# Paired score search in two early slots, and four steps moved in the opening of a fused top-k attention and feed-forward kernel

## The chip, the cores and the metric

The kernel runs on one core of a Trainium2 chip, as one launch. The metric is the device time of that launch in microseconds; lower is better.

## The reference

Top-k attention over 8 batches of 8 heads (sequence 576, head size 64) feeds a feed-forward layer over the 4608 resulting rows. All in float32.

```python
scores = scale * np.matmul(q, k.transpose(0, 1, 3, 2))        # (8, 8, 576, 576), scale = 1/8
kth = np.partition(scores, -32, axis=-1)[..., -32:-31]        # the 32nd largest of each row
scores = np.where(scores >= kth, scores, -1e9)
attn = np.exp(scores - scores.max(-1, keepdims=True))
attn = attn / (attn.sum(-1, keepdims=True) + 1e-09)
x = np.matmul(attn, v).transpose(0, 2, 1, 3).reshape(4608, 512)
h = x @ w_in                                                  # 512 -> 2048
out = (h * (1 / (1 + np.exp(-1.702 * h)))) @ w_out            # 2048 -> 512
```

## The kernel before

The work is cut into 144 **slots** (`N`), 18 to a batch. A slot is 128 query rows of a pair of heads, so its scores `sc` are 128 partitions x 2 heads x 576 keys; two of the 18 take the last 64 rows of two pairs instead. The order of the instructions on each engine is the order in which the program issues them (a manual schedule); nothing reorders them. Tiles come from rotating pools, so a tile's write waits until the buffer's last user is done: `scp` (4 buffers) holds scores, `raws` (7) raw weight pieces and later `lesser` and `h`, `lefts` (2) the searches' working copies, `ps_t` and `ps_s` (2 each) are in PSUM.

What happens to a slot:

- TensorE multiplies q and k (`scores`, L295); ScalarE copies them out of PSUM, scaled (`copy_scores`, L307).
- VectorE finds the 32nd largest of each row. **Whole** (`topk`, L317 and L320): four rounds of MAX8 (eight largest) and MATCH_REPLACE8 (take them out) over 576 values, for both heads. **Paired** (`topk_of_pairs`, L366 to L378): `pair_up` first takes the larger of key j and key j + 288 into `greater` on VectorE (L336), and GpSimd computes the smaller into `lesser` with integer arithmetic, a subtraction (L339) and, in `pair_rest`, an addition (L349). Four rounds over `greater` and two over `lesser`, 288 values each, and two small reductions (L373, L378) give the same bound.
- GpSimd makes two small values per row: for a whole search `cut` and `low` (L410, L411, in `bounds`), for a paired one `low` alone (L399, in `lows`; `cut` comes from L378).
- ScalarE masks with `cut` (L423) and takes exponentials with `low` (L431), summing into `den`.
- VectorE inverts `den` (`invert`, L439 and L441). In the first slots (`divide`) GpSimd puts the inverse on a diagonal `by` (L448) that TensorE multiplies with while it transposes (`turn_main`, `turn_ends`, L468 and L471, copied out by ScalarE at L476); later (`normalize`) GpSimd multiplies the row (L454), ScalarE splits it into 16-bit halves (`split`, L490) and a DMA transposes it (`turn_by_dma`, L492 and L498).
- TensorE multiplies with v (L526 in `values`, L557 in `values_at`); ScalarE copies x out (L539, or L571 and L574). In the first slots `bring_all` issues those copies that were put off, and then the first multiplication with x.

Four slots with all heads of the same rows make a block of x. A unit of the feed-forward layer is: TensorE's `hidden` (L618), ScalarE's `tanh` (L640, and with `aside` a copy `h`, L643), `gate` on VectorE (L655) or, with `aside`, on GpSimd (L652, L653), and TensorE's `project` (L673), written out by `leave` (L681, L683). Units stand in queues (`to_gate`, `gated`, `to_project`), so a unit is projected some slots after its gate.

The weights are rounded in 32 **pieces** in slots 0 to 11: per piece ScalarE's `size`, `low`, `sign` (L151, L154, L153), VectorE's `shift` (L152), and two GpSimd passes, `add` and `finish` (L144, L147), taken from the list `unfinished` by `finish_one`. `project` reads a piece only once it is finished.

Slots 0 to 10 (`slot(n)`, `SETTLED` = 10) use the whole search, and from slot 11 (`PAIRED`) on `two_slots(n)` does two slots at a time with the paired search: `find` searches, `measure` computes `low`, ends the pair build and gates a unit.

Of the kernel before, what the change touches and what calls it, by code (L numbers as in the profile page):

```python
# [11 lines left out]
F32 = mybir.dt.float32  # L12
# [6 lines left out]
P = 128  # L19
# [11 lines left out]
def kernel(  # L31
# [52 lines left out]
    TURNS = 4  # L84
    SETTLED = 10
    PAIRED = SETTLED + 1
    assert D == 64 and 2 * TAIL == P and C == NP * P and C == PIECE and B % 2 == 0
    assert TOPK == 32 and NP == 4 and NF == 4 and NG == 4 and CC == 4

# [219 lines left out]
    def topk(n):  # L309

        sc = st[n]["sc"]
        top = st[n]["top"] = small.tile([P, 2, TOPK], F32, name="top")
        left = [lefts.tile([P, S], F32, name="left") for _ in range(2)]
        of = lambda r, i: left[i][:] if r else sc[:, i, :]

        def largest(r, i):
            nc.vector.max(top[:, i, 8 * r : 8 * r + 8], of(r, i))  # L317

        def remove(r, i):
            nc.vector.match_replace(left[i][:], top[:, i, 8 * r : 8 * r + 8], of(r, i), LOWEST)  # L320

        ops = []
        for r in range(TOPK // 8):
            ops += [lambda r=r, i=i: largest(r, i) for i in range(2)]
            if r < TOPK // 8 - 1:
                ops += [lambda r=r, i=i: remove(r, i) for i in range(2)]
        return ops
# [3 lines left out]
    def pair_up(n):  # L331

        sc = st[n]["sc"]
        a, b = sc[:, :, 0:HALF], sc[:, :, HALF:S]
        greater[n] = lefts.tile([P, 2, HALF], F32, name="greater", tag="left")
        nc.vector.tensor_tensor(out=greater[n][:], in0=a, in1=b, op=ALU.max)  # L336
        lesser[n] = raws.tile([P, 2, HALF], F32, name="lesser", tag="raw")
        whole = lesser[n][:].bitcast(I32)
        nc.gpsimd.tensor_tensor(out=whole, in0=a.bitcast(I32), in1=greater[n][:].bitcast(I32), op=ALU.subtract)  # L339
        unpaired.append(n)  # L340
# [3 lines left out]
    def pair_rest():  # L344

        while unpaired:
            n = unpaired.pop()
            whole, b = lesser[n][:].bitcast(I32), st[n]["sc"][:, :, HALF:S]
            nc.gpsimd.tensor_tensor(out=whole, in0=whole, in1=b.bitcast(I32), op=ALU.add)  # L349

    def topk_of_pairs(n):

        top = st[n]["top"] = small.tile([P, 2, 2 * TOPK], F32, name="top2", tag="top")
        cut = st[n]["cut"] = small.tile([P, 2], F32, name="cut")
        first, few = greater.pop(n), lesser.pop(n)
        left = lefts.tile([P, 2, HALF], F32, name="left2", tag="left")

        def found(r, i, written=False):
            if r < TOPK // 8:
                at = (8 * r + TOPK) % (TOPK + TOPK // 2)  # L360
                return top[:, i, at : at + 8]
            end = 2 * TOPK - 8 * (r - TOPK // 8) - TOPK
            return top[:, i, end - 1 : end - 9 : -1] if written else top[:, i, end - 8 : end]

        def largest(src, r, i):
            nc.vector.max(found(r, i, True), src[:, i, :])  # L366

        def remove(to, src, r, i):
            nc.vector.match_replace(to[:, i, :], found(r, i), src[:, i, :], LOWEST)  # L369

        def merge():
            both = top[:, :, 0:TOPK].rearrange("p i (s k) -> p i k s", s=2)
            nc.vector.tensor_reduce(  # L373
                out=top[:, :, TOPK + TOPK // 2 :], in_=both, axis=mybir.AxisListType.X, op=ALU.max
            )

        def bound():
            nc.vector.tensor_reduce(  # L378
                out=cut[:], in_=top[:, :, TOPK + TOPK // 2 - 1 :], axis=mybir.AxisListType.X, op=ALU.min, negate=True
            )  # L380

        ops = []
        for r in range(TOPK // 8):
            ops += [lambda r=r, i=i: largest(left if r else first, r, i) for i in range(2)]
            if r < TOPK // 8 - 1:
                ops += [lambda r=r, i=i: remove(left, left if r else first, r, i) for i in range(2)]
        ops += [lambda: pair_up(n + 1) if n + 1 < N else None]
        for r in range(TOPK // 8, TOPK * 3 // 16):
            ops += [lambda r=r, i=i: largest(few, r, i) for i in range(2)]
            if r == TOPK // 8:  # L390
                ops += [lambda r=r, i=i: remove(few, few, r, i) for i in range(2)]
        return ops + [merge, bound]
# [9 lines left out]

    def bounds(n):

        if n >= PAIRED:
            return lows(n)
        top = st[n]["top"]
        cut = st[n]["cut"] = small.tile([P, 2], F32, name="cut")
        low = st[n]["low"] = small.tile([P, 2], F32, name="low")
        nc.gpsimd.tensor_scalar(cut[:], top[:, :, TOPK - 1], -1.0, None, op0=ALU.mult)  # L410
        nc.gpsimd.tensor_tensor(out=low[:], in0=top[:, :, TOPK - 1], in1=top[:, :, 0], op=ALU.subtract)  # L411

    def exponentials(n, between=lambda: None):

        mask(n)
        between()
        exps(n)
# [398 lines left out]
    def slot(n):  # L816

        todo = later.pop(n, [])
        for fn, args in todo:
            if fn is not prepare and fn is not prepare_by_dma:  # L820
                fn(*args)
        preparing = [(fn, args) for fn, args in todo if fn is prepare or fn is prepare_by_dma]
        some = [round_piece(x) for x in by_slot.get(n, [])] if n else early
        if n == 0:
            for piece in some:
                piece["low"]()
                piece["sign"]()
        else:
            bounds(n - 1)
            exponentials(n - 1, bring_all if n % 4 == 1 else lambda: None)  # L830
            copy_scores(n + 1)
            bring_all()
            while signs:
                signs.pop(0)()
            if 1 < n <= TURNS:
                turn_main(n - 2)
                turn_ends(n - 2)
            for piece in some:
                piece["size"]()
            tanh(False)  # L840
        for i, op in enumerate(topk(n)):
            op()
            if i == 2:
                for _ in range(min(3 if n >= TURNS else 6, len(unfinished))):
                    finish_one()
            if i == 5:
                if n > 0:
                    divide(n - 1)
                while unfinished:
                    finish_one()  # L850
            if i == 10:
                gate(False)
        if n == SETTLED:
            pair_up(n + 1)
            pair_rest()
        for piece in some:
            piece["shift"]()
            unfinished.extend(piece["finish"])
        if n < NP:
            for fn, args in preparing:  # L860
                fn(*args)
        if n >= TURNS:
            turn_main(n - 1)
            turn_ends(n - 1)
        if n > 0:
            for piece in some:
                piece["low"]()
        scores(n + 2)
        if n == SETTLED:
            copy_scores(n + 2)  # L870
        if n == 0:
            return
        for i, piece in enumerate(some):
            if n == TURNS and i > 0:
                signs.append(piece["sign"])
            else:
                piece["sign"]()
        idle = not ready and n < TURNS
        if 1 < n <= TURNS:
            values(n - 2, put_off if n == TURNS else None)  # L880
        if n >= TURNS:
            values(n - 1, put_off)
        if n >= NP:
            for fn, args in preparing:
                fn(*args)
        if n > PROJECTS and may_project(2):
            project(n == SETTLED)
        if idle:
            stay_warm(8)
        hidden()  # L890
# [12 lines left out]
    def two_slots(n):  # L903
# [27 lines left out]
        def measure(m):  # L931
            if live(m):
                lows(m)
            pair_rest()
            gate(aside)

        def project_one():
            if may_project(0):
                project(True)

        if opens:
            bounds(n - 1)
            gate(aside)
        if ahead:
            scores(n + 2)
# [26 lines left out]
        for piece in some:  # L972
            piece["shift"]()
            piece["low"]()
            piece["sign"]()
            unfinished.extend(piece["finish"])
        if live(n - 1):
            split(n - 1)
        begin(todo[0])
# [26 lines left out]
        find(n + 1)  # L1006
        if live(n):
            normalize(n)
            split(n)
        begin(todo[1])  # L1010
        if live(n):
# [44 lines left out]
```

## Time and profile before

| | |
|---|---|
| median of 3 runs | 1456.52 us (1456.08 to 1456.63) |
| profiled execution, its own time | 1456.39 us |
| its span in the profile | 1454.6 us |
| mean granted TensorE clock | 0.986 |
| busy: TensorE, VectorE, ScalarE, GpSimd | 1416.5, 1362.5, 1158.9, 977.6 us |
| slot 1 starts on VectorE | 19.72 us |
| slot 11 starts on VectorE | 134.65 us |
| last TensorE wait of over 1 us ends | 224.90 us |

In rows of an engine in order of time, the first number is the start in us, the second the length, then engine, line, operation, what it writes and reads, and in brackets how long the engine had been idle before it and what ended that. Instructions of an engine overlap a little at their ends, so the text takes the step from one start to the next as an instruction's price ("steps"). The time outside the span, 1.79 us here, lies before the first and behind the last instruction.

### The profile page before, as it was taken

Reading aid. Unit: us, or ns where it says so; the run is one execution under the profiler, and the core shown is the slowest. Engines: PE = TensorE matmul, PEld = TensorE weight load, DVE = VectorE, ACT = ScalarE, POOL = GpSimd, SP = SyncE. Lnnn points to the kernel's source line nnn. Section 1 sums busy time; section 2 is a strip of 40 time slices with the busy share of each in tenths; the row PEclk is TensorE's granted clock in tenths of the full one; section 3 lists DMA queues with packets and bytes.
Section 4 is the critical chain, followed back from the end, with each engine's and each line's share of the span. In section 5 each row is a group of like instructions: output and inputs, shape, how many; then the busy total and the mean of one; then the engine's idle time right before and its main releaser. Section 6 shows DMA issues by size and latency. Waiting matters only on the chain.

```text
span 1454.6 us, 29079 instructions
## 1 busy us (share of the span) xinstructions
PE 1416.5 (97%) x9524; PEld 996.4 (68%) x9524; DVE 1362.5 (94%) x4681; ACT 1158.9 (80%) x1862; POOL 977.6 (67%) x1177
## 2 busy tenths in 40 slices
PE   7789799999999999999999999999999999999998
PEld 5667466777666667777666667777666667777665
DVE  7999999999999999999999999999999999999910
ACT  6998787888888887888888888888878888777730
POOL 3788766766677777666777777766777767667610
PEclk8899899999999999999999999999999999999999
DMA  7442467777777867777677767767677776645430
GB/s 224 136 161 75 127 154 191 189 189 180 176 198 184 188 170 191 186 198 177 170 194 182 183 170 195 202 174 189 166 203 189 180 182 179 161 133 130 138 89 15
DMA packets 521272, 244.40 MB, mean 168 GB/s; under 512 B 457376, under 2 KB 495264, under 8 KB 521120
## 3 DMA queue, kind: packets, MB, share of 16 engines
q1 hardware_dynamic: 520688, 242.25, 64.4%
q8 instruction: 75, 1.23, 0.3%
q14 instruction: 77, 0.63, 0.2%
q10 hardware_dynamic: 432, 0.30, 0.1%
HBM read 45.09 MB, written 103.42 MB: 102 GB/s over the span
## 4 chain that ended last, share of the span: by engine, by line
PE 87%; DVE 10%; ACT 2%; POOL 0%; issue 0%; DMA 0%; DVEq 0%; POOLq 0%; ACTq 0%
PE ph L618 33%; PE po L673 32%; PE o L557 10%; PE s_ps L295 10%; DVE top L317 4%; DVE left L320 3%; DVE top L366 1%; DVE left L369 1%; ACT sc L490 0%; ACT sc L423 0%; ACT pr L431 0%; DVE wout L152 0%; PE none L169 0%; ACT sc L307 0%; DMA pt<-rows 0%
## 5 line engine op out<-in xcount | busy, mean ns | idle before, releaser
L618 PEld LDWEIGHTS ph<-xT,win 128*128 128x128 f32 x3520 | 484.2, 191 | 85.2 <-issue 54.6
L618 PE MATMUL ph<-xT,win 128*128 128x128 f32 (+1 forms) x3520 | 537.1, 309 | 0.5 <-ACT xT L574 0.5
L673 PE MATMUL po<-wout,th 128*128 128x512 f32 x1152 | 521.0, 595 | 5.6 <-POOL wout L147 5.6
L490 ACT COPY sc<-pr 128x2304 uint16<-128x2304 uint16 x134 | 283.1, 2113 | 170.3 <-POOL pr L454 170.3
L673 PEld LDWEIGHTS po<-wout,th 128*128 128x128 f32 x1152 | 213.6, 191 | 219.0 <-issue 205.8
L366 DVE MAX8 top<-left 128x8 f32<-128x288 f32 x798 | 323.2, 446 | 0.0
L339 POOL TENSOR_TENSOR lesser<-sc,greater 128x576 int32<-128x576 int32 x133 | 188.4, 1417 | 179.8 <-DVE greater L336 179.8
L454 POOL TENSOR_SCALAR pr<-pr,rden 128x576 f32<-128x576 f32 x268 | 196.6, 746 | 126.7 <-DVE top L373 77.7
L369 DVE MATCH_REPLACE8 left<-top,left 128x288 f32<-128x288 f32 x532 | 231.3, 442 | 0.0
L431 ACT ACTIVATE pr<-sc,low 128x576 f32<-128x576 f32 x288 | 220.8, 774 | 0.0
L366 DVE MAX8 top<-lesser 128x8 f32<-128x288 f32 x532 | 214.9, 445 | 0.0
L423 ACT ACTIVATE sc<-sc,cut 128x576 f32<-128x576 f32 x288 | 207.4, 774 | 6.2 <-POOL cut L410 6.2
L307 ACT ACTIVATE sc<-s_ps 128x576 f32<-128x576 f32 x288 | 170.9, 648 | 34.2 <-PE s_ps L295 32.6
L349 POOL TENSOR_TENSOR lesser<-lesser,sc 128x576 int32<-128x576 int32 x133 | 187.8, 1412 | 0.1
L295 PE MATMUL s_ps<-qk_t 64*128 64x288 f32 (+1 forms) x1280 | 183.7, 433 | 0.5 <-ACT qk_t L218 0.3
L653 POOL TENSOR_TENSOR th<-th,h 128x512 f32<-128x512 f32 x131 | 167.5, 1279 | 10.9
L295 PEld LDWEIGHTS s_ps<-qk_t 64*128 64x128 f32 (+1 forms) x1280 | 100.2, 179 | 79.2 <-issue 59.0
L557 PE MATMUL o<-pt,v_l 128*64 128x128 f32 (+1 forms) x2400 | 145.8, 265 | 2.1 <-DMA pt<-rows 1.9
L557 PEld LDWEIGHTS o<-pt,v_l 128*64 128x64 f32 x2400 | 121.4, 137 | 29.5 <-issue 17.7
L336 DVE TENSOR_TENSOR greater<-sc 128x576 f32<-128x576 f32 x133 | 131.9, 992 | 0.0
L652 POOL TENSOR_SCALAR th<-th 128x512 f32<-128x512 f32 x131 | 81.5, 622 | 59.7 <-ACT th L640 59.7
L640 ACT ACTIVATE th<-ph 128x512 f32<-128x512 f32 x144 | 85.5, 593 | 38.0 <-PE ph L618 33.9
(78 smaller groups left out, 1365.5 us busy)
## 6 DMA issues: line engine op xcount, KB each, us to landing
rows<-sc SPq DMA_DIRECT2D x134, 576.0 KB, 3.2
qk_rows<-halves SPq DMA_DIRECT2D x48, 256.0 KB, 2.8
qk_l<-in_q_dram SPq DMA_DIRECT2D x64, 128.0 KB, 3.4
raw<-in_moe_w_in_dram SPq DMA_DIRECT2D x16, 512.0 KB, 4.7
v_l<-in_v_dram SPq DMA_DIRECT2D x32, 256.0 KB, 3.7
raw<-in_moe_w_out_dram SPq DMA_DIRECT2D x16, 512.0 KB, 3.5
out_dram<-ob SPq DMA_DIRECT2D x32, 256.0 KB, 2.9
qk_l<-in_k_dram SPq DMA_DIRECT2D x62, 128.0 KB, 3.4
```

The lines of the kernel that those rows point to most:

```text
L295: nc.tensor.matmul(ps[i][rows, c, 0:HALF], lhsT=qT[b, hps[p]][on, cols], rhs=kT[b, hps[p]][on, FIRST[i] + c * HALF : FIRST[i] + (c + 1) * ...
L339: nc.gpsimd.tensor_tensor(out=whole, in0=a.bitcast(I32), in1=greater[n][:].bitcast(I32), op=ALU.subtract)
L349: nc.gpsimd.tensor_tensor(out=whole, in0=whole, in1=b.bitcast(I32), op=ALU.add)
L366: nc.vector.max(found(r, i, True), src[:, i, :])
L369: nc.vector.match_replace(to[:, i, :], found(r, i), src[:, i, :], LOWEST)
L423: nc.scalar.activation(sc[:, i, :], sc[:, i, :], AF.Prelu, bias=cut[:, i : i + 1], alpha=HUGE)
L431: nc.scalar.activation(pr[:, i * S : (i + 1) * S], sc[:, i, :], AF.Exp, bias=low[:, i : i + 1], accum_out=den[:, i : i + 1],)
L454: nc.gpsimd.tensor_scalar(pr[:, i, :], pr[:, i, :], st[n]["rden"][:, i : i + 1], 1.0, op0=ALU.mult, op1=ALU.mult)
L490: nc.scalar.copy(out=halves, in_=pr[:].bitcast(U16).rearrange("p (k h) -> p h k", h=2))
L557: nc.tensor.matmul(o[j * D : (j + 1) * D, cols], lhsT=main[:, j, c, :] if c < NF else tail[:, j, :], rhs=pt[:, MAIN[j] + c if c < NF else ...
L618: nc.tensor.matmul(ph[:, i * many * P : (i + 1) * many * P], lhsT=win[:, c, f * P : (f + 1) * P], rhs=xs[:, first : first + step * (many - ...
L673: nc.tensor.matmul(x.po[:], lhsT=gT[:, i * P : (i + 1) * P], rhs=wout[:, f, :], start=(x.done == 0), stop=(x.done == FC - 1))
```

## The change

Slots 1 and 2 (`EARLY`) use the paired search, with `lesser` in a buffer of `scp`; `bounds` of the slot before a paired one is issued ahead of the pair build, also for slot 10. In those two slots the inversion (`divide`) comes after the eleventh step of the search, and so do the last finishing passes ahead of L448. In slot 5 (`TURNS + 1`) the put-off copies of x come behind the exponentials, not between mask and exponentials, and the gate comes after the last step of the search. In slot 4 (`TURNS`) two of the three `low` steps on ScalarE are issued ahead of the transposes. In the first pair of slots (11, 12) two finishing passes take the place of a gate ahead of the end of the pair build, slot 11's own piece is finished right behind, and the gates follow one slot later. In slot 13 `tanh` is issued ahead of `split`. The order of TensorE's instructions and of SyncE's is not changed.

```diff
+    EARLY = (1, 2)
+    by_pairs = lambda n: n in EARLY or PAIRED <= n < N
...
-        lesser[n] = raws.tile([P, 2, HALF], F32, name="lesser", tag="raw")
+        home, tag = (scp, "sc") if n in EARLY else (raws, "raw")
+        lesser[n] = home.tile([P, 2, HALF], F32, name="lesser", tag=tag)
...
-        ops += [lambda: pair_up(n + 1) if n + 1 < N else None]
+        ops += [lambda: pair_up(n + 1) if PAIRED < n + 1 < N else None]
...
-        if n >= PAIRED:
+        if by_pairs(n):
             return lows(n)
...
-            bounds(n - 1)
-            exponentials(n - 1, bring_all if n % 4 == 1 else lambda: None)
+            if not by_pairs(n):
+                bounds(n - 1)
+            exponentials(n - 1, bring_all if n % 4 == 1 and n > TURNS + 1 else lambda: None)
+            if n == TURNS + 1:
+                bring_all()
...
-        for i, op in enumerate(topk(n)):
+        for i, op in enumerate(topk_of_pairs(n) if n in EARLY else topk(n)):
...
-            if i == 5:
+            if i == (10 if n in EARLY else 5):
                 if n > 0:
                     divide(n - 1)
                 while unfinished:
                     finish_one()
-            if i == 10:
+            if i == (13 if n == TURNS + 1 else 10):
                 gate(False)
-        if n == SETTLED:
+        if by_pairs(n + 1):
+            bounds(n)
             pair_up(n + 1)
             pair_rest()
...
+        lows_of = [piece["low"] for piece in some] if n > 0 else []
+        if n == TURNS:
+            for _ in range(2):
+                lows_of.pop(0)()
         if n >= TURNS:
             turn_main(n - 1)
             turn_ends(n - 1)
-        if n > 0:
-            for piece in some:
-                piece["low"]()
+        for low in lows_of:
+            low()
...
             if live(m):
                 lows(m)
+            if opens and m == n:
+                finish_one()
+                finish_one()
+                pair_rest()
+                return
             pair_rest()
             gate(aside)
+            if m == SETTLED + 4:
+                gate(aside)
...
         if opens:
-            bounds(n - 1)
             gate(aside)
...
             unfinished.extend(piece["finish"])
+        while unfinished:
+            finish_one()
         if live(n - 1):
             split(n - 1)
...
             normalize(n)
+        if n == SETTLED + 3:
+            tanh(aside)
+        if live(n):
             split(n)
```

## The prediction

> **What bounds the kernel now.** I read the page's busy table and its 40 slices first, then the chain that ended last, then each engine in order of time through the first 230 us, since the diff ends at slot 14 (about 185 us).
>
> ```profile
> PE 1416.5 (97%) x9524; PEld 996.4 (68%) x9524; DVE 1362.5 (94%) x4681; ACT 1158.9 (80%) x1862; POOL 977.6 (67%) x1177
> PE   7789799999999999999999999999999999999998
> DVE  7999999999999999999999999999999999999910
> PEclk8899899999999999999999999999999999999999
> PE 87%; DVE 10%; ACT 2%; POOL 0%; issue 0%; DMA 0%; DVEq 0%; POOLq 0%; ACTq 0%
> ```
>
> TensorE is full from the sixth slice on: after 225 us it waits 0.5 us in all. Its instruction order is the same in both kernels, so a gain must come from waits before 225 us, and what is gained there is kept to the end. In the opening VectorE (DVE) carries the chain, slot after slot, with only these two waits in slots 1 to 10:
>
> ```profile
> 68.37 0.17 DVE L439 TENSOR_SCALAR some<-den 128x2 f32<-128x2 f32 x1 [1.06 <-ACT pr L431]
> 72.77 0.69 DVE L655 SCALAR_TENSOR_TENSOR th<-th,ph 128x512 f32<-128x512 f32 x1 [0.54 <-ACT th L640]
> ```
>
> Both are in slot 5. The busy time by slot shows why (first number the length, then PE, PEld, DVE, ACT, POOL): ScalarE (ACT) works 13.22 of 13.30 us in slot 5 and 11.42 of 11.51 in slot 6. It is a second bound right behind DVE.
>
> ```profile
> 63.13:76.43 13.30, 12.07 (x131) 10.39 (x128) 11.66 (x27) 13.22 (x28) 9.24 (x11) 0.99 0.45 146
> 76.43:87.94 11.51, 9.17 (x86) 7.96 (x86) 11.47 (x27) 11.42 (x24) 9.14 (x9) 1.00 0.40 138
> ```
>
> Behind slot 10 the chain goes through GpSimd (POOL) to ACT and back to DVE, and TensorE has its last large gaps:
>
> ```profile
> 156.03 1.41 POOL lesser L339
> 157.44 1.45 POOL pr L454 x2
> 158.91 2.11 ACT sc L490
> ...
> 164.40 0.23 DVE some L439
> ```
> ```profile
> 153.52 2.07 PE L673 MATMUL po<-wout,th 128*128 128x512 f32 x2 [5.07 <-POOL wout L147]
> 156.13 2.07 PE L673 MATMUL po<-wout,th 128*128 128x512 f32 x2 [0.53 <-POOL wout L147]
> 179.50 0.66 PE L217 MATMUL tp<-ident,qk_l 128*128 128x128 f32 x4 [1.01 <-ACT h L643]
> 224.90 1.09 PE L557 MATMUL o<-pt,v_l 128*64 128x128 f32 x16 [1.33 <-DMA pt<-rows]
> ```
>
> **Part 1: paired search in slots 1 and 2.** Slot 1's whole search runs 19.72 to 29.64 us with 0.27 of L439/L441 in it: 9.65. Slot 11's paired search steps 1.57 three times and 0.73 (5.45), then 2.64 for lesser, merge and bound (152.25 to 155.20 less 0.31): 8.09. L336, new in front of it, steps 0.66 with POOL quiet. So 0.90 less per slot, 1.80 for two.
>
> Against it stands POOL. L336 and L439 wait while a POOL instruction runs:
>
> ```profile
> 150.72 1.60 DVE L336 TENSOR_TENSOR greater<-sc 128x576 f32<-128x576 f32 x1
> 160.65 0.74 DVE L336 TENSOR_TENSOR greater<-sc 128x576 f32<-128x576 f32 x1
> ```
>
> The first meets L144 (150.43 to 151.71), the second a free POOL. Following POOL's queue: cut(0) and low(0) end at 20.7 (the shifts L152 hold them back, as at 40.39), L339 and L349 (1.41 each) to 23.5, four piece passes (1.3 each) to 28.8, two L448 to 29.45. lesser is needed at 25.8, so it is covered by 2 us. L439 of slot 1 falls at a seam between pieces (24.7, costs 0.15). At the end of slot 1, L448 delays the second L336 by about 0.3; low(1), behind it and the two shifts, comes at 31.2, half a microsecond after the mask is done, and L339 and L349 after that push the pieces so that slot 2's L439 meets one (0.4 to 0.6). Ends of this cost: 0, or 1.3 for each of two L336 and two L439 (5.2). I take 0.8, near the rows' phase: part 1 brings **-1.0** at the start of slot 3.
>
> The Trainium skill ("SBUF — State Buffer", section "Who interferes with whom") says that a DVE instruction with two SBUF inputs and a GpSimd one that reads SBUF block each other for the whole instruction, which speaks against adding L336 and four passes of 1.41 here. The 1.60 agrees. Were every added pass met whole, part 1 would lose: -1.8 + 4 x 1.41 = +3.8.
>
> **Part 2: slot 5.** Two L154 of slot 4 move ahead of the second turn, where ACT waits 0.59 and 1.12 for TensorE; so the mask starts at 63.9, not 65.0. x's copy (0.37) moves behind the exponentials. Together den is ready at 66.75, and L439 wants it at 67.2: the 1.06 is gone. The gate moves to the last place, 73.2, and tanh is done at 71.7: the 0.54 is gone. **-1.60.** What is late next: x's copy comes 0.7 later, TensorE's L618 behind it starts at 67.15 and ends 70.8, so ACT now waits 0.4 for the transposes, and slot 6's mask starts 76.9 instead of 77.4. DVE has moved by 2.6 there, ACT by 1.5 (0.5 plus the 1.0 of part 1, since slot 4's mask follows DVE's cut). Mask and exponentials take 2.9: den at 76.9 - 1.0 + 2.9 = 78.8, L439 at 80.53 - 2.6 = 77.9. DVE waits: **+0.9** (bounds 0 and 2.3). After that DVE's 11.5 a slot is longer than ACT's 11.05, and the lag shrinks. Sum at slot 11: -1.0 - 1.6 + 0.9 = **-1.7**.
>
> **Part 3: bounds ahead, two pieces ahead of a gate** (times of before, on top of -1.7). bounds(10) ahead of the pair build frees ACT's mask 1.75 earlier (135.96 against 137.71), but the next copy waits for scores at 141.6 anyway: nothing, cover 2.8. On POOL, slot 10's third piece goes ahead of L349 at 147.1 and is done at 149.75 (before: 153.46), slot 11's piece at 154.5 (156.07). The gate (L652, L653, 1.9) goes one slot back. Hence L454 of slot 11 starts at 156.0, not 157.41, L490 at 157.5, and L439, which waited 1.43 at 164.40, does not wait for den. But L336 at 160.2 now meets L653 (160.0 to 161.25) and pays about 0.7. The unit gated late is read only at 183.67, two units lie ahead of it: no wait. Net for DVE **-0.85** (bounds 0 and -1.9).
>
> **Part 4: tanh ahead of the split.** ph is there at 172.95, tanh and h end at 174; L490 waits for L454 until 175.5 anyway, so the split pays nothing (cover 1.5). TensorE loses its 1.01 and stands 1.4 + 1.0 earlier at 187, where pt of slot 13 (DVE -0.85, landing 4.5 after its issue at 183.72) holds it about 0.2. With L490 earlier, L653 leaves L336 at 180.40 alone (1.26 to 0.74), and DVE's wait of 0.88 at 202.80, which goes back to TensorE's L673 through L681, goes too: both stand at about **-2.2** at 209, where DVE waits for TensorE's scores. From there the chain to 224.90 moves as a whole.
>
> On the clock: the profile's 3 us stretches show TensorE granted 1.00 from 90 to 93 us with a wait of 2.09, then 0.69 and 0.74, and 0.50 from 155 to 161 after the 5.07. In its place come gaps of about 1.3 and 2.7, and I leave the slow stretch in; TensorE has 1 us to spare before pt of slot 11 there. "TensorE: Matmul & The Clock Gate" (Part 1) puts the throttle after an idle window of about 3.4 us; the 2.09 does not fit that. By the page TensorE would be some 4 us better off in this stretch, and the sum the same, since DVE is last.
>
> **Sum.** -1.7 - 2.2 = -3.9. The profiled execution took 1456.39 with a span of 1454.6 (1.79 around it): 1452.5. It lies 0.13 under the median 1456.52, from which -3.9 gives 1452.6.
>
> **Rivals.** *ACT keeps the opening.* For it: 11.42 of 11.51 us busy. If low(1), and the exponentials and score copy queued behind it, cost ACT 1.4 us more in slots 2 to 5, slot 6 hands back 2.3 for 0.9, and parts 1 and 2 leave 0.3; with parts 3 and 4 at -1.9 that is -2.2: 1454.3. Against it: the mask of slot 4 is bound by DVE's cut. Chance 0.19, from 0 to -2.9.
> *TensorE, not DVE, sets the way to 225 us*, with no collisions: -1.7 (a full part 1, 0.1 kept back), -1.6, +0.8, and -3.5 (1.5 + 1.0 + 0.45 at L222 + part of the 1.33): -6.0, 1450.5. Against it: DVE is busy 9.57 of 9.67 at 175 to 184. Chance 0.14.
> *Slower: DVE falls into another rhythm with POOL.* From 290 to 1380 us L336 alternates 1.25 and 0.74 in each pair of slots of 18.87, and in stretches of 100 us DVE is 98.2 to 99.1 busy: 0.2 idle a pair. If a changed phase makes both 1.25, it owes 0.51 - 0.2 = 0.3 in each of 61 pairs: +19, less 4: 1471. It decides as soon as the second L336 of a pair meets more than 0.2 of a POOL pass. Against it: the last reduce L378 leads TensorE's next scores by 1.4 us at 300 and 1.7 at 1200, so the rhythm is set by TensorE. Chance 0.07.
> That an edit does nothing: the order of the instructions shows them all in place; part 4 alone could be idle, which is inside the range.
>
> **How the numbers follow.** The sum holds: 0.60, from -2.9 to -5.2, 1451.3 to 1453.6. A change under 0.2%, 2.9 us, is about what a measurement of this kernel cannot tell from none. Faster by more: 0.60 + 0.14 = 0.74; within: 0.19; slower: 0.07. The range goes from -6.3 to -1.2: it leaves out the slow rival, the low end of ACT's (0.06) and the far end of TensorE's (0.03).
>
> **What would show it.** Right: no wait at L439 and L655 in slot 5, one of about 1 us at L439 in slot 6; slot 11's L366 near 133 instead of 134.65; wout waits of under 3 us; no wait at L217 near 176; TensorE full from about 221. Wrong: L439 or L336 of slots 1 and 2 over 1 us; ACT waits in slots 5 to 7 that DVE pays for; L336 at 1.25 twice in a pair after 225.

## The result, and the profile after

| | before | after |
|---|---|---|
| median | 1456.57 us (1456.05 to 1457.44, 12 runs) | 1452.59 us (1452.07 to 1453.72, 12 runs) |
| profiled execution, its own time | 1456.39 us | 1453.04 us |
| its span | 1454.6 us | 1451.2 us |

The ratio is 0.9974, with a 95% interval of 0.9965 to 0.9982: 3.98 us faster, inside the predicted range and 0.01 us from the predicted time. The way there is not quite the predicted one: the opening gave 0.7 more than the sum had, and a late transfer at 241 us took 0.9 of it back in the profiled execution.

The page of the changed kernel first (lines have moved down by two or three: L336 is L338, L378 is L381, L431 is L434, L439 is L442, L557 is L560, L655 is L658, L673 is L676):

```profile
PE 1414.1 (97%) x9524; PEld 995.2 (69%) x9524; DVE 1361.8 (94%) x4703; ACT 1159.9 (80%) x1862; POOL 985.2 (68%) x1181
PE   7889899999999999999999999999999999999998
DVE  7999999999999999999999999999999999999910
PEclk8999999999999999999999999999999999999999
PE 85%; DVE 11%; ACT 1%; DMA 1%; SPq 1%; issue 1%; POOL 0%; DVEq 0%; POOLq 0%
```

GpSimd has four instructions and 7.6 us of work more. The second and the fifth slice of TensorE are each a tenth fuller, and the clock's low second and fifth slice (the fifth is 145 to 181 us) are gone. The chain now has a DMA share of 1%, which is new: three transfers of `pt` stand in it, issued at 159.95, 180.02 and 235.53 (4.67, 5.26 and 5.37 us), where before there was one, at 220.33 (4.53).

VectorE in order of time, the rows that the prediction named:

```profile
44.38 0.49 DVE L442 TENSOR_SCALAR some<-den 128x2 f32<-128x2 f32 x1
66.55 0.15 DVE L442 TENSOR_SCALAR some<-den 128x2 f32<-128x2 f32 x1
72.36 0.67 DVE L658 SCALAR_TENSOR_TENSOR th<-th,ph 128x512 f32<-128x512 f32 x1
78.07 0.17 DVE L442 TENSOR_SCALAR some<-den 128x2 f32<-128x2 f32 x1
132.28 0.81 DVE L369 MAX8 top<-greater 128x8 f32<-128x288 f32 x2
148.95 1.57 DVE L338 TENSOR_TENSOR greater<-sc 128x576 f32<-128x576 f32 x1
158.96 0.74 DVE L338 TENSOR_TENSOR greater<-sc 128x576 f32<-128x576 f32 x1
161.19 0.16 DVE L442 TENSOR_SCALAR some<-den 128x2 f32<-128x2 f32 x1
177.14 0.74 DVE L338 TENSOR_TENSOR greater<-sc 128x576 f32<-128x576 f32 x1
198.59 0.17 DVE L442 TENSOR_SCALAR some<-den 128x2 f32<-128x2 f32 x1 [0.46 <-ACT pr L434]
```

Both waits of slot 5 are gone (66.55, 72.36 have no bracket). At 78.07, in slot 6, there is none either, where about 1 us was predicted. Slot 11 begins at 132.28 instead of 134.65. At 158.96 L338 takes 0.74: the collision that the sum charged 0.7 for did not come in this profile (in the second profile of the same kernel, after_again, it did: 1.27). Another one came that the sum does not have, at the shift in front of slot 12's search, here before, and after with the GpSimd pass that it met:

```profile
144.94 0.42 DVE L152 TENSOR_SCALAR wout<-wout 128x512 uint32<-128x512 uint32 x1
```
```profile
142.61 0.97 DVE L154 TENSOR_SCALAR wout<-wout 128x512 uint32<-128x512 uint32 x1
142.56 1.62 POOL L457 TENSOR_SCALAR pr<-pr,rden 128x576 f32<-128x576 f32 x2
```

The wait of 1.43 that L439 had at 164.40 is gone (161.19), L338 at 177.14 is short, and of the 0.88 near 200 us 0.46 is left. In exchange the small L442 at 44.38 takes 0.49: it stands in a GpSimd pass (43.56 to 44.84).

The same two slots as before, busy time by slot, and then four of the 3 us stretches (length, PE, PEld, DVE, ACT, POOL, and behind them the granted clock, the DMA share and GB/s):

```profile
61.45:72.94 11.49, 10.94 (x118) 9.37 (x116) 11.46 (x27) 11.30 (x25) 9.84 (x12) 1.00 0.46 157
72.94:84.50 11.56, 9.14 (x94) 7.94 (x92) 11.53 (x28) 11.48 (x24) 8.80 (x8) 1.00 0.42 139
...
90.00:93.00 3.00, 2.46 (x13) 2.46 (x14) 3.00 (x7) 2.90 (x7) 2.88 (x4) 0.67 0.36 132
...
150.00:153.00 3.00, 1.29 (x2) 0.30 (x2) 3.00 (x10) 1.86 (x4) 3.00 (x2) 0.91 0.24 59
153.00:156.00 3.00, 3.00 (x13) 1.93 (x13) 2.93 (x14) 1.06 (x1) 2.58 (x6) 0.52 0.74 156
156.00:159.00 3.00, 2.01 (x10) 1.06 (x9) 3.00 (x12) 3.00 (x5) 2.62 (x3) 1.00 0.36 149
```

The stretches from 153 us in the kernel before:

```profile
153.00:156.00 3.00, 2.07 (x2) 0.50 (x2) 2.93 (x15) 0.71 (x2) 2.92 (x3) 0.50 0.71 157
156.00:159.00 3.00, 2.87 (x6) 1.23 (x8) 3.00 (x12) 0.09 (x1) 3.00 (x5) 0.50 0.20 45
159.00:162.00 3.00, 3.00 (x14) 2.10 (x13) 3.00 (x10) 3.00 (x3) 2.92 (x5) 0.50 0.05 20
```

Slot 5 is 11.49 us long instead of 13.39, both counted from shift to shift, and ScalarE fills 11.48 of slot 6's 11.56: the two engines run side by side with nothing to spare. Behind 150 us one 3 us stretch is near half clock where there were three.

TensorE in order of time:

```profile
90.54 3.38 PE L471 MATMUL tp<-xT,pr 128*128 128x128 f32 x16 [1.93 <-POOL xT L451]
147.34 1.12 PE L676 MATMUL po<-wout,th 128*128 128x512 f32 x2 [0.70 <-POOL wout L149]
151.71 1.39 PE L676 MATMUL po<-wout,th 128*128 128x512 f32 x2 [3.25 <-POOL wout L149]
220.66 1.09 PE L560 MATMUL o<-pt,v_l 128*64 128x128 f32 x16 [1.30 <-DMA pt<-rows]
240.94 1.09 PE L560 MATMUL o<-pt,v_l 128*64 128x128 f32 x16 [0.89 <-DMA pt<-rows]
```

The 5.07 and 0.53 for wout have become 0.70 and 3.25, and the 1.01 at L217 has no row any more. The wait that ended at 224.90 ends at 220.66, 4.24 earlier. Then a wait appears that had been 0.03 (at 244.29): 0.89 at 240.94. So 4.24 - 0.86 = 3.38 reach the end, as the spans say (3.4).

### The profile page after: what moved, and what is told of

It reads as the page before. It is cut to its first block, busy times and chain, and to the rows that moved or that the text cites. A ratio compares the mean times of both kernels' runs of the same rounds, so it can differ in the third digit from the quotient of the medians.

```text
span 1451.2 us, 29107 instructions
## 1 busy us (share of the span) xinstructions
PE 1414.1 (97%) x9524; PEld 995.2 (69%) x9524; DVE 1361.8 (94%) x4703; ACT 1159.9 (80%) x1862; POOL 985.2 (68%) x1181
## 4 chain that ended last, share of the span: by engine, by line
PE 85%; DVE 11%; ACT 1%; DMA 1%; SPq 1%; issue 1%; POOL 0%; DVEq 0%; POOLq 0%
PE ph L621 33%; PE po L676 31%; PE o L560 10%; PE s_ps L297 10%; DVE top L319 3%; DVE left L322 3%; DVE top L369 2%; DVE left L372 1%; DMA pt<-rows 1%; DVE greater L338 0%; ACT sc L493 0%; DVE lesser L372 0%; DVE wout L154 0%; POOL pr L457 0%; DVE win L154 0%
## 5 line engine op out<-in xcount | busy, mean ns | idle before, releaser
L676 PE MATMUL po<-wout,th 128*128 128x512 f32 x1152 | 519.3, 593 | 4.9 <-POOL wout L149 3.9
L676 PEld LDWEIGHTS po<-wout,th 128*128 128x128 f32 x1152 | 213.0, 190 | 217.8 <-issue 205.1
L369 DVE MAX8 top<-left 128x8 f32<-128x288 f32 x810 | 328.0, 446 | 0.0
L457 POOL TENSOR_SCALAR pr<-pr,rden 128x576 f32<-128x576 f32 x268 | 196.4, 745 | 127.4 <-DVE top L376 76.8
L372 DVE MATCH_REPLACE8 left<-top,left 128x288 f32<-128x288 f32 x540 | 234.8, 442 | 0.0
L434 ACT ACTIVATE pr<-sc,low 128x576 f32<-128x576 f32 x288 | 220.8, 773 | 0.0
L369 DVE MAX8 top<-lesser 128x8 f32<-128x288 f32 x540 | 218.0, 444 | 0.0
L656 POOL TENSOR_TENSOR th<-th,h 128x512 f32<-128x512 f32 x131 | 167.6, 1279 | 11.2 <-POOL th L655 0.4
L560 PE MATMUL o<-pt,v_l 128*64 128x128 f32 (+1 forms) x2400 | 145.9, 265 | 3.7 <-DMA pt<-rows 3.5
L560 PEld LDWEIGHTS o<-pt,v_l 128*64 128x64 f32 x2400 | 121.4, 137 | 31.3 <-issue 16.9
L338 DVE TENSOR_TENSOR greater<-sc 128x576 f32<-128x576 f32 x135 | 133.2, 986 | 0.0
L655 POOL TENSOR_SCALAR th<-th 128x512 f32<-128x512 f32 x131 | 80.9, 617 | 58.8 <-ACT th L643 58.8
```

The source lines that it names most:

```text
L434: nc.scalar.activation(pr[:, i * S : (i + 1) * S], sc[:, i, :], AF.Exp, bias=low[:, i : i + 1], accum_out=den[:, i : i + 1],)
L457: nc.gpsimd.tensor_scalar(pr[:, i, :], pr[:, i, :], st[n]["rden"][:, i : i + 1], 1.0, op0=ALU.mult, op1=ALU.mult)
L560: nc.tensor.matmul(o[j * D : (j + 1) * D, cols], lhsT=main[:, j, c, :] if c < NF else tail[:, j, :], rhs=pt[:, MAIN[j] + c if c < NF else ...
L676: nc.tensor.matmul(x.po[:], lhsT=gT[:, i * P : (i + 1) * P], rhs=wout[:, f, :], start=(x.done == 0), stop=(x.done == FC - 1))
```

## The experiments

"Against before" is a ratio to the unchanged kernel's runs on the same chip, with its 95% interval. Positions inside the opening are counted from the end of slot 0, since that falls at 18.4 to 19.9 us from run to run; so counted, the changed kernel stands at -1.17 after slots 1 and 2, -0.73 after slot 3, and -2.50 at slot 11 (all against the kernel before).

Two measures of scatter belong beside what follows. The unchanged kernel's own runs on the chips of the experiments lie between 1454.3 and 1458.0 us, so a difference of well under 1 us between two medians shows nothing by itself. And kernels whose instructions have the same order up to the end of slot 10's search do not always stand alike at slot 11: the unchanged opening stood at +0.09, -0.32 and +0.64 in later_only, p3_only and p4_only; the changed one at -2.48 to -2.50 in four profiles and at -1.40 in opening_only. One profile's position at slot 11 is good to about 1 us.

**p1_only.** Part 1 alone.

```diff
+    EARLY = (1, 2)
+        for i, op in enumerate(topk_of_pairs(n) if n in EARLY else topk(n)):
```

> The kernel before with the paired search in slots 1 and 2 alone (and the order of bounds that goes with it). Landmarks: start of slot 11's search on VectorE (before 134.65, the change 132.28) and the last reduce of slot 19 (222.50 and 218.28). Theory 'parts are chained through ScalarE': slot 3 starts 0.9 earlier, but ScalarE moves by only 0.6 in slots 3 to 5 (in the change its mask of slot 3 moved from 52.31 to 51.72), so the wait at the inversion in slot 5 grows from 1.06 to about 1.3 and slot 11 starts 0.6 earlier, 134.05; total 1456.0. Rival 'parts add': slot 11 at 133.7, total 1455.6. Rival of the prediction's first part gone wrong (collisions with GpSimd): slot 3 not earlier at all.

1457.12 us, against before 1.0004 (0.9994 to 1.0013). After slots 1 and 2 it stood at -1.17, slot 3 took 0.44 back, and -0.72 was still there at slot 11; the waits of slot 5 stayed as they were. So the size was right and the total shows none of it. TensorE's trace says where it went: waits of 1.42 at 223.66 and 1.58 at 244.51 for pt.

**p2_only.** Part 2 alone.

```diff
+            exponentials(n - 1, bring_all if n % 4 == 1 and n > TURNS + 1 else lambda: None)
+            if n == TURNS + 1:
+                bring_all()
...
+            if i == (13 if n == TURNS + 1 else 10):
...
+        if n == TURNS:
+            for _ in range(2):
+                lows_of.pop(0)()
```

> The kernel before with the steps in slots 4 and 5 alone (two low steps ahead of the second turn, copies of x behind the exponentials, the gate last). Theory: both waits of slot 5 (1.06 and 0.54) go and the inversion of slot 6 comes at 78.93 with den ready at about 78.6, so no wait follows: slot 11 at 133.05, total 1454.9. Rival as the prediction had it: ScalarE hands 0.9 back at the inversion of slot 6: slot 11 at 133.9, total 1455.8.

1455.88 us, against before 0.9992 (0.9983 to 1.0001). Slot 5 lost 1.89 with both waits gone, and slot 6 took nothing back. ScalarE's debt came four slots later and was small:

```profile
124.58 0.17 DVE L442 TENSOR_SCALAR some<-den 128x2 f32<-128x2 f32 x1 [0.30 <-ACT pr L434]
```

At slot 11 it stood at -1.44.

**p3_only.** Part 3 alone (with bounds of slot 10 ahead of the pair build, and slot 11's own piece finished right behind).

```diff
+            if opens and m == n:
+                finish_one()
+                finish_one()
+                pair_rest()
+                return
...
+            if m == SETTLED + 4:
+                gate(aside)
```

> The kernel before with the order of slots 10 to 14 alone (bounds ahead of the pair build, two pieces ahead of a gate, gates one slot later). Slot 11 starts as before, 134.65. Theory: VectorE's wait of 1.43 at 164.40 goes, slot 14's end is 0.9 earlier, the contended larger-of-two step at 180.40 gets 0.5 shorter, but TensorE keeps its wait of 1.01 for the copy h: slot 19 0.9 to 1.4 earlier, total 1455.4. Rival: the gates later on GpSimd hit VectorE's larger-of-two step and nothing is left: 1456.5.

1456.31 us, against before 0.9995 (0.9986 to 1.0005). On VectorE -0.89 from slot 11 to 13 and -0.90 to 19, where -0.85 was predicted.

**p4_only.** Part 4 alone.

```diff
+        if n == SETTLED + 3:
+            tanh(aside)
```

> The kernel before with one tanh ahead of the split of slot 13 alone. Slot 11 as before. Theory 'VectorE is last': TensorE's wait of 1.01 at 179.50 goes, but VectorE is not earlier by more than its 0.88 wait at 202.80; slot 19 0 to 0.6 earlier, total 1456.2. Rival 'TensorE is last there': slot 19 1.0 earlier, total 1455.5. Rival 'the split is late': tanh waits for its matmuls and delays the split by up to 1, total 1457.

1456.20 us, against before 0.9996 (0.9987 to 1.0005). VectorE -0.59 from slot 11 to 15 and -0.80 to 19; L219's wait is gone.

On VectorE the four come to 0.72 + 1.44 + 0.90 + 0.80 = 3.86, for 2.50 + 1.85 = 4.35 in the changed kernel, which is as near as the scatter allows; their medians, against the 1456.81 of the kernel before beside them, come to only 1.7. Two kinds of run follow this up, halves of the change and the transfer that TensorE waits for.

**opening_only** and **later_only.** Parts 1 and 2, and parts 3 and 4.

```diff
 # opening_only, against the changed kernel (the rest of parts 3 and 4 likewise)
-            if opens and m == n:
-                finish_one()
-                finish_one()
...
-        if n == SETTLED + 3:
-            tanh(aside)
```
```diff
 # later_only, against the changed kernel (the rest of part 2 likewise)
-    EARLY = (1, 2)
+    EARLY = ()
...
-        if n == TURNS:
-            for _ in range(2):
-                lows_of.pop(0)()
```

> Parts 1 and 2 together, parts 3 and 4 as in the kernel before. In the runs of one part alone, parts 1 and 2 stood at -0.72 and -1.44 behind slot 10, yet their medians were +0.6 and -0.8 against the kernel before; all four together gave -4.0. Theory A (the single runs were blurred by transfers that land at different times, and the parts add): -2.5 behind slot 10, nothing more up to slot 19, 1454.2. Theory B (a single gain is eaten by a wait that only goes when later parts help TensorE too): -2.5 behind slot 10, but 1455.5 or more, with TensorE waits of over 1 us for pt behind 220 us.

> Parts 3 and 4 together, parts 1 and 2 as in the kernel before. Theory A (the parts add): nothing up to slot 10, -1.7 to -1.9 from slot 11 to 19, 1454.9. Theory B (only both halves together move TensorE): under 1 us of gain, 1455.8 or more.

opening_only: 1456.17 us, against before 1.0001 (0.9992 to 1.0010). later_only: 1454.04 us, 0.9983 (0.9975 to 0.9992). Neither theory holds as put. On VectorE opening_only stood at -1.4 at slot 11 (not -2.5: waits of 0.47 in slot 6 and 0.31 in slot 10 for ScalarE) and kept it to slot 19; later_only gained 2.8 between them, more than parts 3 and 4 apart. TensorE's rows, of opening_only and then of later_only:

```profile
223.12 1.09 PE L560 MATMUL o<-pt,v_l 128*64 128x128 f32 x16 [1.33 <-DMA pt<-rows]
244.33 1.09 PE L560 MATMUL o<-pt,v_l 128*64 128x128 f32 x16 [1.85 <-DMA pt<-rows]
```
```profile
222.48 1.09 PE L560 MATMUL o<-pt,v_l 128*64 128x128 f32 x16 [1.43 <-DMA pt<-rows]
```

opening_only reached 223.12, 1.78 ahead of before, and lost 1.85 at 244.33. later_only had no second wait and kept its 2.42. That opening_only stands 1.1 short of the changed kernel at slot 11, with the same order of instructions up to there, is scatter that is not explained. This is theory B's wait, but not for B's reason: it does not go when TensorE is helped, it goes when one transfer lands soon. The table sets the transfer out for every profiled run (in every row but the last two the span less the sum of the first two numbers is 1229.6 to 1229.9, so these two decide the time; after_again has a slow stretch of TensorE besides, and turn_first later waits):

| run | first wait ends | second wait | span | transfer takes | instruction packets meanwhile |
|---|---|---|---|---|---|
| before | 224.90 | 0.03 | 1454.6 | 4.5 | 0 |
| later_only | 222.48 | 0 | 1452.3 | 4.6 | 0 |
| p3_only | 224.60 | 0.22 | 1454.7 | 4.7 | 0 |
| without1 | 220.70 | 0.23 | 1450.7 | 4.8 | 0 |
| p4_only | 225.24 | 0.59 | 1455.6 | 5.1 | 0 |
| p2_only | 222.94 | 0.75 | 1453.3 | 5.2 | 0 |
| after | 220.66 | 0.89 | 1451.2 | 5.4 | 1 |
| turn_early | 220.08 | 0 | 1450.0 | 5.4 | 1 |
| lows_late | 222.15 | 1.29 | 1453.0 | 5.8 | 1 |
| early3 | 222.66 | 1.32 | 1453.8 | 5.8 | 1 |
| p1_only | 223.66 | 1.58 | 1454.9 | 6.1 | 2 |
| opening_only | 223.12 | 1.85 | 1454.6 | 6.3 | 2 |
| after_again | 220.45 | 0 | 1451.6 | 5.5 | 1 |
| turn_first | 219.80 | 0 | 1454.0 | 4.7 | 1 |

In each row with a second wait, the transfer's time less that wait is 4.4 to 4.6: what the transfer takes beyond about 4.5 us is paid whole. (turn_early and turn_first issue it 2 us earlier, and in after_again TensorE itself comes later, so none of the three waits.)

The last column is from the DMA view, asked for the time from the issue of the transfer to its landing. For later_only, the changed kernel and opening_only in turn (the first line is the rate in 40 equal slices, the others the queues: packets, MB, share):

```profile
GB/s 135 137 128 179 232 204 159 179 179 91 58 51 97 137 97 102 142 159 192 230 248 263 268 230 281 296 288 285 285 294 299 288 285 374 325 361 460 336 495 195
```
```profile
GB/s 191 120 195 147 162 210 122 99 67 38 114 164 139 151 185 183 198 215 107 261 217 36 27 13 10 8 8 82 286 296 284 296 284 296 284 290 499 336 427 473
...
q14 instruction: 1, 0.01, 0.9%
```
```profile
GB/s 58 92 126 270 288 202 156 86 55 105 95 110 180 180 165 86 91 123 322 191 31 8 8 6 8 108 291 288 290 294 286 291 438 388 401 414 644 201 375 408
...
q14 instruction: 2, 0.02, 0.6%
```

In later_only the middle runs through at over 200 GB/s. In the other two the rate falls to 36 and less for six slices of 5.37/40 us and five of 6.33/40 us, about 0.8 us in both, and a queue that carries instructions, not data, has moved a packet just ahead of it (at 237.5 to 238.2 in the changed kernel, the standstill begins at 238.3). p1_only, after_again and lows_late have such a standstill behind a packet too. In the table no transfer without a packet took over 5.2 us, none with one under 5.4 but turn_first's 4.7, and the two with two took 6.1 and 6.3. It is not the packet alone: turn_early, early3 and turn_first had one and no standstill (5.4, 5.8, 4.7), and in p2_only the rate fell to 14, 8 and 18 GB/s for about 0.4 us with no such packet in the window (5.2). Nothing was run that moves the packet by itself, so the cause of the late landing, and what decides when a packet comes, stay open; that the landing decides what is kept of the gain is what the table shows.

**after_again.** The changed kernel itself, once more.

> The changed kernel itself, once more, as the yardstick for the runs beside it. If the wait of TensorE for a transposed transfer near 241 us (0.03 in the profile of before, 0.89 in that of after, 0.22 to 1.58 in the four kernels with one part each) is scatter of the transfer's landing, it differs again here; if it belongs to the change, it is 0.9 again. Total 1452.6.

1452.70 us, against before 0.9974 (0.9964 to 0.9984): the result repeats. This time VectorE gained 2.59 from slot 11 to 19 (1.85 in the first profile). Most of the difference lies in slots 11 to 13: the shift in front of slot 12 took 0.44 (0.97 in the first profile), L338 in slot 12 0.95 (1.57), L338 in slot 13 1.27 (0.74), in all 0.62 less. The second wait did not come; but the first, 1.82 long, was followed by a slow stretch (16 matmuls of L560 took 1.81 us, not 1.09).

**without1.** Part 1 alone undone.

```diff
-    EARLY = (1, 2)
+    EARLY = ()
```

> Part 1 alone undone (slots 1 and 2 search the whole scores again), all else as in the changed kernel. If part 1 adds its -0.7 to whatever else is there: slot 11 starts 0.7 later than in the changed kernel, 1453.3. If part 1 is worth nothing in the total, as its run alone had it (+0.6): 1452.6.

1453.64 us, against before 0.9983 (0.9974 to 0.9992): 1.05 more than the changed kernel's 1452.59. The median sides with the first theory; the intervals overlap, so that the difference is not 0 is not shown. Its profile has -1.44 at slot 11, 1.06 less than the changed kernel and as much as p2_only; but opening_only, which has part 1, stands at -1.40, so that the positions do not settle it either.

**lows_late.** The two low steps of slot 4 back behind the transposes.

```diff
-        if n == TURNS:
-            for _ in range(2):
-                lows_of.pop(0)()
```

> The changed kernel without the two low steps moved ahead of the second turn of slot 4 (slot 5's other steps stay). Theory 'ScalarE is a second bound right behind VectorE': its mask of slot 4 comes about 1.0 later (63.6 for 62.63); in the change den is ready 0.04 before the inversion of slot 6 asks for it, so the inversions of slots 5 and 6 together wait about 0.9 and slot 11's search starts 0.9 later, 133.2; total 1453.5. Rival 'ScalarE has slack': slot 11 at 132.3, total 1452.6.

1453.81 us, against before 0.9980 (0.9971 to 0.9990): 1.1 more than after_again on the same chip, with intervals that overlap. VectorE's waits for den came back:

```profile
66.80 0.17 DVE L442 TENSOR_SCALAR some<-den 128x2 f32<-128x2 f32 x1 [0.68 <-ACT pr L434]
79.27 0.17 DVE L442 TENSOR_SCALAR some<-den 128x2 f32<-128x2 f32 x1 [0.86 <-ACT pr L434]
114.09 0.17 DVE L442 TENSOR_SCALAR some<-den 128x2 f32<-128x2 f32 x1 [0.19 <-ACT pr L434]
```

1.73 in these three and 2.1 in all at slot 11 (1.0 against opening_only). ScalarE is the second bound of the opening, as argued; in four of the five profiles of the changed opening the two steps just keep it ahead.

**early3.** A third early paired slot.

```diff
-    EARLY = (1, 2)
+    EARLY = (1, 2, 3)
```

> The changed kernel with slot 3 searching paired too. Slot 3 has three pieces: GpSimd's queue there is 2.8 for the pair build, 7.8 for six passes, 0.7 and 0.5, in all 11.8, against 10.2 us of VectorE's slot. Theory 'GpSimd and ScalarE are full there': the low values come late, slot 4's mask with them, slot 11's search starts 0 to 1 us later than in the change (132.3 to 133.3) although VectorE's own work is 0.9 less; total 1452.6 to 1453.6. Rival 'VectorE alone bounds the opening': slot 11 at 131.4, total 1451.7.

1455.53 us, against before 0.9990 (0.9981 to 1.0000). Slot 3 got 0.91 shorter, but slot 4 took 13.79 instead of 10.92. VectorE in slot 4, and GpSimd beside its first row:

```profile
49.62 3.27 DVE L154 TENSOR_SCALAR win<-win 128x512 uint32<-128x512 uint32 x3
56.91 0.83 DVE L442 TENSOR_SCALAR some<-den 128x2 f32<-128x2 f32 x1
```
```profile
49.54 1.29 POOL L146 TENSOR_TENSOR win<-win,raw 128x512 int32<-128x512 int32 x1
50.91 1.36 POOL L149 TENSOR_TENSOR win<-win,raw 128x512 f32<-128x512 f32 x1
```

Three shifts that take 1.08 elsewhere took 3.27 with two GpSimd passes over them, and L442 took 0.83 instead of 0.16: 2.86 of the 2.87. A whole search makes GpSimd wait for its cut at a slot's end (1.16 us idle at 50.70 in the changed kernel), and the shifts begin in that gap, ahead of the cut (which then takes 0.98); a paired one makes no such gap. It is a loss of the kind that the prediction bounded part 1 with, one slot further on.

**turn_first** and **turn_early.** The slot's own transfer ahead of the next loads on SyncE's queue, in all pairs and in those up to slot 23.

```diff
 # turn_first
-        begin(todo[1])
         if live(n):
             turn_by_dma(n)
+        begin(todo[1])
```
```diff
 # turn_early
+        if n > 2 * SETTLED + 3:
+            begin(todo[1])
         if live(n):
             turn_by_dma(n)
+        if n <= 2 * SETTLED + 3:
+            begin(todo[1])
```

> The changed kernel with the loads of the pair's second slot queued behind the transposing transfer, not ahead of it. In the change's profile the transfer that TensorE waits for at 240.94 is issued at 235.53, right behind 4.2 us of loads in SyncE's queue, though its rows were written out at 230.95 and take about 3 to land. Theory 'the queue holds it': it is issued at about 234, the wait at 241 goes, 0.3 to 0.9 less than the changed kernel: 1452.0. Rival 'landing scatter alone': the wait stays, 1452.6. Rival 'loads late': values or queries come late and TensorE waits elsewhere, over 1453.5.

> The changed kernel, with the slot's own rows and transfer ahead of the second lot of loads on SP's queue in slots up to 23 only; from slot 25 on the loads go first again. If those loads, as in the changed kernel, are what make the transfer of slot 21 late (issued at 235.53, 5.37 to land), and if the later waits of the kernel with all slots swapped came from its late slots: no wait near 241 nor behind 260, 1451.7. If the landing scatters whatever the order: 1452.6, the same as the changed kernel.

turn_first: 1454.20 us, against before 0.9983 (0.9975 to 0.9992), slower than the changed kernel by median. Its transfer went out at 233.23 instead of 235.53 and the wait near 241 was gone, but a later slot paid:

```profile
316.97 1.61 PE L560 MATMUL o<-pt,v_l 128*64 128x128 f32 x16 [2.00 <-DMA pt<-rows]
```

turn_early: 1452.01 us, against before 0.9971 (0.9961 to 0.9981). It has one TensorE wait for pt behind 220 us and none after:

```profile
220.08 1.09 PE L560 MATMUL o<-pt,v_l 128*64 128x128 f32 x16 [1.00 <-DMA pt<-rows]
```

The transfer still took 5.4; it began 2 us earlier (233.51). So the loads ahead of it in the queue set when it begins, and the landing scatters whatever the order: each expectation had half. It beats the kernel before; that it beats the changed one (0.58 by medians, not on the same chip) is likely and not shown, since the intervals overlap.

## Why the prediction was right, and where it was not

- **Part 1 (-1.0).** Right in size: -1.17 at the start of slot 3, where -1.0 was put, and -0.73 behind slot 3, in two runs. The collisions were put into slots 1 and 2; 0.44 came in slot 3 instead: L442 at 44.38 (0.49 instead of 0.16) and the shifts in front (1.18 instead of 1.08). One row was misread: at 160.65 L336 did not meet a free GpSimd. GpSimd's L652 began at 160.69 and took 1.18 instead of 0.61, so there GpSimd was the one held up.
- **Part 2 (-1.60, then +0.9).** The first number came out at -1.90. The second is the step that failed: "x's copy comes 0.7 later ... slot 6's mask starts 76.9 instead of 77.4", less part 1's 1.0, put the mask at 75.9 and den at 78.8. The mask started at 75.09, 0.8 earlier: 0.27 of it was there in slot 4 already (62.63 for 63.9 - 1.0), 0.2 is ScalarE's wait for the transposes (0.19, not 0.4), and the rest was not taken apart. So den was there at 78.03, 0.04 ahead of VectorE. The margin was that thin: lows_late shows 0.86 lost at the same place, opening_only 0.47, p2_only nothing there and 0.30 four slots later. The sum at slot 11 was -2.4 on the clock of the trace, not -1.7; opening_only, with 0.47 of the forecast 0.9, came out at -1.7.
- **Part 3 (-0.85).** -0.89 from slot 11 to 13 in the changed kernel and alone, but right by luck. Of its terms, the 1.43 at L439 went as forecast (with the 0.7 that makes -0.73; the other 0.12 of the -0.85 has no row behind it). The 0.7 was not paid, since L656 ended at 158.70, 0.26 ahead of L338; in its place the shift in front of slot 12 paid 0.55, a collision that the sum does not have. L338 at 148.95 still met a pass (1.57), as in the kernel before. Of the nine profiles with part 3, five show -0.88 or -0.89; in the other four (after_again, later_only, turn_first, turn_early) the 0.5 at slot 13's L338 is paid, the shift and slot 12's L338 are short, and part 3 brings -1.5. The two go apart at that shift, by who comes first: within 0.02 us of GpSimd's L457, in those four, it takes 0.42 to 0.44; 0.05 to 0.20 behind it, in the five, 0.82 to 0.97.
- **Part 4.** The wait at L217 went and L338 at 177.14 is short, as predicted; the 0.88 went only by half. The transfer of slot 13, put at 4.5, took 5.26 and held TensorE 0.48 at 185.33, not 0.2. Parts 3 and 4 gave -1.85 and -2.59 in the two profiles, for -2.2.
- **"From there the chain to 224.90 moves as a whole."** It did, by 4.24. The step left out is the next transfer: TensorE arrived at it with 0.03 of a wait before, so any microsecond won ahead of it could be lost there if it landed late. The prediction has no term for it, and for the one transfer that it prices it has a fixed 4.5; this one took 4.5 to 6.3. In the profiled execution this returned 0.86, and in opening_only all of 1.78.
- So the total of 3.98 is close partly by luck: the opening gave 0.7 more than the sum had, parts 3 and 4 in the profiled execution 0.35 less, and the transfer took back 0.9 there.
- **Clock.** The slow stretch that was left in the sum shrank from three stretches of 0.50, 153 to 162, to one of 0.52 at 153 to 156. VectorE is last there, and nothing of it shows in the end. The wout waits were put at 1.3 and 2.7, with "under 3 us" as a sign of being right; they were 0.70 and 3.25, so that this sign failed. The slow stretch at 90 us remained, 0.67 behind a wait of 1.93. The Trainium skill ("TensorE: Matmul & The Clock Gate", Part 1) puts the throttle after an idle window of about 3.4 us; the 3.25 is close to that, the 1.93 is not, so that the page's figure does not fit here either.
- **Rivals.** ScalarE did not keep the opening, though in lows_late it kept 2.1 of it. TensorE did not set the way to 225 us on its own (4.24 there, not 6.0). The other rhythm of VectorE and GpSimd did not come: behind 225 us L338 alternates 1.25 and 0.74 as before.

## What to carry to other kernels

Follow a gain past the stage where it is made, to the next place where the bound engine arrives with no margin: a wait of 0.03 is a bound already there, and for a transfer the spread of its landing belongs in the price. When one engine's waits are taken out, compare the second engine's busy time with the new length (11.48 of 11.56 here): without two small steps moved, lows_late stood 2.1 us later at slot 11 and 1.1 later by medians. A cheaper algorithm on one engine can also take away the gap in which that engine used to run undisturbed: the third paired slot saved 0.91 and cost 2.87.

## What the runs showed of the hardware

- In five profiles, the changed kernel's and opening_only's among them, the DMA rate fell to under 40 GB/s for 0.7 to 0.8 us behind a packet on a queue that carries instructions; the profile counts 77 such packets of 8 KB on q14 in the run. The Trainium skill ("Runtime: NRT & Kernel Launch", section "Instruction fetch mechanics") calls the cost of fetching the next block of instructions "mostly hidden". In the table a transfer that TensorE waits for took 5.4 to 6.3 us with such packets beside it and 4.5 to 5.2 without, but 4.7 with one in turn_first, and p2_only had a shorter fall of the rate without one: the two meet, and whether one makes the other is not shown.
- VectorE's smallest instruction, 128 x 2, is held up by a GpSimd pass as a large one is: 0.49 and 0.83 instead of 0.16. GpSimd is held up as well: L652 beside L336 took 1.18 instead of 0.61 in the kernel before. Hundredths of a microsecond decide which: in all fourteen profiles the shift ahead of slot 12 takes 0.41 to 0.44 where it starts within 0.02 us of GpSimd's first pass of L457 (L454 in the kernel before), and 0.82 to 0.97 where it starts 0.05 to 0.21 later.
- A wait of 1.82 us was followed by a slow clock (in after_again, L560 1.81 instead of 1.09, granted 0.78 and 0.65 in the 3 us stretches from 219 us) and one of 1.85 in opening_only was not (1.09, granted 1.00): the length of one wait does not decide it.
